# Attention and W1 of the next batch woven into the G2 matmuls of this batch, in one fixed order for all engines

## The chip, the core and the metric

The kernel runs on one core of one Trainium2 chip. The time is the device time of one execution in microseconds (us); several executions are taken and the median is quoted. The record gives with each run the span of the core, from its first to its last instruction, which is 1.7 to 1.9 us shorter than the time. Every ratio with an interval is the mean time of one kernel's fast runs over that of the other's fast runs of the same rounds, so it is not quite the ratio of the medians that stand beside it. A run over 1.5% above the fastest of its kernel counts as slow and is left out of the ratios.

In the profile's lines, PE is the TensorE matmul, PEld its weight load, DVE the VectorE, ACT the ScalarE, POOL the GpSimd and SP the SyncE. A "q" after an engine's name is its sequencer. L279 is line 279 of the kernel in question. PEclk is the granted TensorE clock as a share of full speed, and a "slot" is a stretch for which it was granted.

## The reference

Eight batches, eight heads, 512 rows of x and 32 rows of state per head, 64 values per row. Attention goes both ways between x and state (`xread`, `sread`). The heads are then concatenated to 512 columns, and every row goes through a two-layer network with SiLU.

```python
scores  = 0.125 * x @ state.T;  xread = softmax(scores)  @ state
scores2 = 0.125 * state @ x.T;  sread = softmax(scores2) @ x
x_moe = concat([xread, sread], axis=rows), heads side by side   # 8 * 544 rows x 512
h = x_moe @ w_in          # 512 x 2048
g = h * sigmoid(h)        # SiLU
out = g @ w_out           # 2048 x 512, float32
```

Both kernels use that xread of a batch is `a @ state`, with `a` the 512 x 32 softmax of a head. So `xread @ w_in` is `a @ (state @ w_in)`. The product W1 = state @ w_in (heads and state rows together: 256 rows x 2048 columns) is made once per batch; then G1 is a @ W1 with a contraction of 256 instead of 512, SiLU follows on ACT, and G2 is the product with w_out. The sread rows of all batches (256 rows) go through w_in directly, as one last group. W1 needs only state and w_in; it does not need the attention.

## The kernel before

It has two stages. The first does attention for 16 groups (a batch and half of its heads each) and W1 four groups later. The second does G1, SiLU and G2 for one batch after the other, with four output banks open at once. A scheduler orders the instructions.

```python
def c_part(b, hg, evict_split):                      # W1 of half a batch
    for fb in range(4):
        w1_psum = psC.tile([128, 512], FP32, tag="w1ps")
        for j in range(2):                           # two tiles of 64 columns
            nc.tensor.matmul(w1_psum[ds(64 * j, 64), :], stateT_bd[:, b, hg, j, :],
                w_in_sb[:, 2 * hg + j, ds(512 * fb, 512)], start=True, stop=True,
                tile_position=(0, 64 * j))
        ...                                          # eviction: 3 on DVE, 1 on ACT
for g, (b, hg) in enumerate(groups):                 # first stage
    ...   # load x, cast, transpose, scores, EXP, row sums, normalise on POOL, sread, transpose a
    if g >= 4:
        c_part(*groups[g - 4], evict_split=3)
        wout_quarter(g - 4, "pool")                  # cast of a piece of w_out
...
for b in range(B):                                   # second stage
    ...
    for ft in range(16):
        if ft + 1 < 16: emit_silu(ft + 1)
        if ft + 2 < 16: emit_G1(ft + 2)              # 2 matmuls of 512 columns
        emit_G2(ft)                                  # 4 matmuls of 512 columns, 4 banks
    ...                                              # evict and store
...
# the last group's stores: 4 batches outermost, then 32 rows
eng.dma_start(out_sread[ds(4 * tt, 4), ds(512, 32), :], out_sb[:])
```

The softmax here doesn't subtract the row's maximum and nothing guards it: scores larger than these inputs give would overflow.

Of the kernel before, what the change touches and what calls it, by code (L numbers as in the profile page):

```python
# [19 lines left out]
def kernel(  # L20
# [11 lines left out]
    B = 8  # L32
    H = 8
    S = 512
    NS = 32
    D = 64
    DM = 512
    DF = 2048
    SCALE = 0.125

    pers = ctx.enter_context(tc.tile_pool(name="pers", bufs=1))

    ident = pers.tile([128, 128], BF16)
    make_identity(nc, ident)

    stateT_bd = pers.tile([128, B, 2, 2, 64], BF16)
    w_in_sb = pers.tile([128, 4, DF], BF16)
    w_out_sb = pers.tile([128, 16, DM], BF16)
    aT_all = pers.tile([128, B, 2, S], BF16)
    xmoeT_sread = pers.tile([128, 4, B * NS], BF16)  # L50
    W1_sb = pers.tile([128, B, 2, DF], BF16)
    ones_sb = pers.tile([128, 1], BF16)
    nc.vector.memset(ones_sb[:], 1.0)

    win_stage = ctx.enter_context(tc.tile_pool(name="win_stage", bufs=1))
    win_tiles = []
    for kt in range(4):
        t = win_stage.tile([128, DF], FP32, tag=f"win{kt}")
        win_tiles.append(t)

    with tc.tile_pool(name="stA", bufs=1) as stA:
        state_stage = stA.tile([128, B, 2, D], FP32)
        state_nat = stA.tile([128, B, 2, D], BF16)

        for kt in range(4):
            for i in range(2):
                src = state[:, 2 * kt + i, :, :].rearrange("b ns d -> ns b d")
                eng = nc.sync if (2 * kt + i) % 2 == 0 else nc.scalar
                eng.dma_start(state_stage[ds(32 * kt, 32), :, i, :], src)

        for kt in range(4):
            nc.gpsimd.dma_start(win_tiles[kt][:], moe_w_in[ds(128 * kt, 128), :])

        nc.gpsimd.memzero(stateT_bd[:])

        nc.gpsimd.tensor_copy(state_nat[:], state_stage[:])  # L76

        with tc.tile_pool(name="psA", bufs=1, space=bass.MemoryType.PSUM) as psA:
            psum_st = psA.tile([128, B, 2, 2, 32], BF16)
            for b in range(B):  # L80
                nc.tensor.transpose(  # L81
                    psum_st[:, b, :, :, :],
                    state_nat[:, b, :, :],
                    ident[:],
                )
            nc.vector.tensor_copy(
                stateT_bd[ds(0, 64), :, :, :, ds(0, 32)],
                psum_st[ds(0, 64), :, :, :, :],
            )
            nc.scalar.activation(  # L90
                stateT_bd[ds(64, 64), :, :, :, ds(32, 32)],
                psum_st[ds(64, 64), :, :, :, :],
                func=COPY,
                bias=0.0,
            )

    groups = [(b, hg) for b in range(B) for hg in range(2)]
    wout_re = moe_w_out.rearrange("(gg q) m -> q gg m", q=128)

    with tc.tile_pool(name="poolB4", bufs=2) as poolB4, \  # L100
         tc.tile_pool(name="poolB2", bufs=2) as poolB2, \
         tc.tile_pool(name="wout_pool", bufs=2) as wout_pool, \
         tc.tile_pool(name="poolPB2", bufs=2, space=bass.MemoryType.PSUM) as poolPB2, \
         tc.tile_pool(name="poolPB1", bufs=1, space=bass.MemoryType.PSUM) as poolPB1, \
         tc.tile_pool(name="psC", bufs=2, space=bass.MemoryType.PSUM) as psC:

        wout_tiles = {}

        def c_part(b, hg, evict_split):
            for fb in range(4):  # L110
                w1_psum = psC.tile([128, 512], FP32, tag="w1ps")
                for j in range(2):
                    nc.tensor.matmul(  # L113
                        w1_psum[ds(64 * j, 64), :],
                        stateT_bd[:, b, hg, j, :],
                        w_in_sb[:, 2 * hg + j, ds(512 * fb, 512)],
                        start=True,
                        stop=True,
                        tile_position=(0, 64 * j),
                    )  # L120
                dst = W1_sb[:, b, hg, ds(512 * fb, 512)]
                if fb < evict_split:
                    nc.vector.tensor_copy(dst, w1_psum[:])  # L123
                else:
                    nc.scalar.activation(dst, w1_psum[:], func=COPY, bias=0.0)  # L125

        def wout_quarter(qidx, eng):
            g2, q = qidx // 4, qidx % 4
            if eng == "pool":
                nc.gpsimd.tensor_copy(w_out_sb[:, qidx, :], wout_tiles[g2][:, q, :])  # L130
            elif eng == "dve":
                nc.vector.tensor_copy(w_out_sb[:, qidx, :], wout_tiles[g2][:, q, :])
            else:
                nc.scalar.activation(
                    w_out_sb[:, qidx, :], wout_tiles[g2][:, q, :], func=COPY, bias=0.0
                )

        for g, (b, hg) in enumerate(groups):
            if g == 0:
                wout_tiles[0] = wout_pool.tile([128, 4, DM], FP32, tag="wout", name="wout0")  # L140
                nc.sync.dma_start(wout_tiles[0][:], wout_re[:, ds(0, 4), :])
            elif g == 2:
                wout_tiles[1] = wout_pool.tile([128, 4, DM], FP32, tag="wout", name="wout1")
                nc.scalar.dma_start(wout_tiles[1][:], wout_re[:, ds(4, 4), :])
            elif g == 8:
                wout_tiles[2] = wout_pool.tile([128, 4, DM], FP32, tag="wout", name="wout2")
                nc.sync.dma_start(wout_tiles[2][:], wout_re[:, ds(8, 4), :])
            elif g == 12:
                wout_tiles[3] = wout_pool.tile([128, 4, DM], FP32, tag="wout", name="wout3")
                nc.scalar.dma_start(wout_tiles[3][:], wout_re[:, ds(12, 4), :])  # L150

            if g < 4:
                nc.vector.tensor_copy(w_in_sb[:, g, :], win_tiles[g][:])  # L153

            x_stage = poolB4.tile([128, 2, 4, 2, D], FP32, tag="x_stage")
            x_nat = poolB4.tile([128, 2, 4, 2, D], BF16, tag="x_nat")
            xT_sb = poolB4.tile([128, 2, 4, 128], BF16, tag="xT_sb")
            exp_nat = poolB4.tile([128, 4, 2, 2, 32], BF16, tag="exp_nat")
            rowsumA = poolB4.tile([128, 4, 2, 2, 1], FP32, tag="rowsumA")
            recipA = poolB4.tile([128, 4, 2, 2, 1], FP32, tag="recipA")  # L160

            a_norm = poolB2.tile([128, 4, 2, 2, 32], BF16, tag="a_norm")
            recipB = poolB2.tile([128, 1], FP32, tag="recipB")
            sread_sb = poolB2.tile([128, D], BF16, tag="sread_sb")

            xT_psum = poolPB2.tile([128, 2, 4, 128], BF16, tag="xT_psum")
            scores_psum = poolPB2.tile([128, 4, 2, 2, 32], FP32, tag="scores_psum")
            sread4_psum = poolPB1.tile([128, 65], FP32, tag="sread4_psum")
            trans_psum = poolPB1.tile([128, 5, 2, 2, 32], BF16, tag="trans_psum")

            for hl in range(4):
                jj, ii = hl // 2, hl % 2
                h = 4 * hg + hl
                src = x[b, h].rearrange("(p c) d -> p (c d)", p=128, c=4)
                eng = nc.sync if hl % 2 == 0 else nc.scalar
                eng.dma_start(x_stage[:, jj, :, ii, :], src)

            nc.vector.tensor_copy(x_nat[:], x_stage[:])  # L178

            for j in range(2):  # L180
                for c in range(4):
                    nc.tensor.transpose(  # L182
                        xT_psum[:, j, c, :], x_nat[:, j, c, :, :], ident[:]
                    )

            nc.scalar.activation(xT_sb[:], xT_psum[:], func=COPY, bias=0.0)  # L186

            for c in range(4):
                for j in range(2):
                    nc.tensor.matmul(  # L190
                        scores_psum[:, c, j, :, :],
                        xT_sb[:, j, c, :],
                        stateT_bd[:, b, hg, j, :],
                        start=True,
                        stop=True,
                    )

            nc.scalar.activation(  # L198
# [78 lines left out]
    with tc.tile_pool(name="psD_h", bufs=3, space=bass.MemoryType.PSUM) as psD_h, \  # L277
# [8 lines left out]
        for b in range(B):  # L286
# [45 lines left out]
            for ft in range(16):  # L332
                if ft + 1 < 16:
                    emit_silu(ft + 1)
# [55 lines left out]
        for ft in range(16):  # L390
            if ft + 1 < 16:
                emit_silu_s(ft + 1)
            if ft + 2 < 16:
                emit_G1_s(ft + 2)
# [40 lines left out]
```

## Time and profile before

| what | value | read from |
|---|---|---|
| time | 307.87 us (three runs, 307.54 to 310.25) | runs |
| span of the profiled run | 311.4 us | page |
| attention and W1, 20 to 122 us | PE busy 73%, clock 0.72 | windows |
| G1 and G2, 123 to 301 us | PE busy 99%, clock 1.00 | windows |
| one 512-column matmul at full clock | 0.216 us from start to start | chain of waits |
| last matmul to end of span | 10.1 us | timeline |

The page of the kernel before: part 1 (busy time and share by engine), two rows of part 2 (40 slices of the span, in tenths) and part 4 (the chain that ended last).

```profile
PE 253.0 (81%) x1638; PEld 123.2 (40%) x1656; DVE 96.5 (31%) x217; ACT 121.7 (39%) x198; POOL 31.8 (10%) x40
...
PE   0015777777878797999999999999999999999960
...
PEclk9999759558655769999999999999999999999995
...
PE 71%; DMA 11%; DVE 5%; POOL 5%; issue 3%; ACT 2%; ACTq 1%; DVEq 0%; SPq 0%; POOLq 0%
```

The windows view of the kernel before, for the two stages. The columns are named in its first line.

```profile
core 0: us, PE busy (x) PEld busy (x) DVE busy (x) ACT busy (x) POOL busy (x), PEclk, DMA share, GB/s
20.00:122.00 102.00, 74.51 (x793) 39.53 (x795) 70.98 (x179) 40.52 (x55) 26.29 (x28) 0.72 0.46 109
123.00:301.00 178.00, 176.56 (x835) 82.75 (x852) 19.88 (x33) 80.43 (x142) 0.00 (x0) 1.00 0.14 48
```

The second stage is full: its time is its matmuls. The first is not: no engine is busy all the time, and where PE pauses, the clock granted to it falls as well, so even its busy time is inflated. What can be gained is in the first 122 us and in the end.

The PE timeline of the kernel before, near the end of the first stage, shows what a pair of W1 matmuls costs (start, duration, engine, line, operation, out<-in, shape, count).

```profile
117.41 0.41 PE L113 MATMUL w_psum<-w_in_sb,stateT_bd 128*64 128x512 bf16 x2
117.75 0.60 PE L298 MATMUL h_psum<-aT_all,W_sb 128*128 128x512 bf16 x2
```

The two W1 matmuls of a pair, on different column tiles, run at the same time; from the start of the pair to the next matmul are 0.34 us, of which 0.216 us is what one 512-column matmul takes; the other 0.12 us comes where the tile shape changes, as matmuls of one shape follow each other at 0.216.

### The profile page before, as it was taken

The page shows a single profiled execution, that of the slowest core. Times are in us where ns is not written, and L with a number is a line of the kernel's source. Part 1 is how long each engine was busy: PE and PEld are TensorE (multiplying, and loading weights), DVE is VectorE, ACT ScalarE, POOL GpSimd, SP SyncE. Part 2 cuts the span into 40 slices and gives each one's busy share as a digit, 9 for nine tenths or more (in the row PEclk, how much of TensorE's full clock was granted, in tenths as well). Part 3 has the DMA queues.
Part 4 walks back from the last instruction along what each step waited for, and adds up shares of the span by engine and source line. Part 5 has one row for each costly group of instructions (what it writes and reads, how often), then busy time and mean ns, then how long its engine had stood idle before and what let it go on. Part 6 is the DMA issues. An engine that isn't in the chain of part 4 may idle for free.

```text
span 311.4 us, 4295 instructions
## 1 busy us (share of the span) xinstructions
PE 253.0 (81%) x1638; PEld 123.2 (40%) x1656; DVE 96.5 (31%) x217; ACT 121.7 (39%) x198; POOL 31.8 (10%) x40
## 2 busy tenths in 40 slices
PE   0015777777878797999999999999999999999960
PEld 0012454443444432444444444444444444445640
DVE  0333677778766866003011030030110300301100
ACT  0021435325423352544435444444354444443430
POOL 5026433212212110000000000000000000000000
PEclk9999759558655769999999999999999999999995
DMA  7998746463533000004004030030030300300301
GB/s 212 378 348 214 163 107 155 98 202 84 119 87 68 2 1 0 0 2 137 0 2 135 0 115 22 0 135 2 1 135 0 119 18 0 137 0 0 138 3 64
DMA packets 43549, 26.50 MB, mean 85 GB/s; under 512 B 36616, under 2 KB 36616, under 8 KB 43016
## 3 DMA queue, kind: packets, MB, share of 16 engines
q1 hardware_dynamic: 21476, 11.01, 12.6%
q10 hardware_dynamic: 21476, 11.01, 12.5%
q0 software_dynamic: 576, 4.19, 3.7%
q8 instruction: 13, 0.21, 0.3%
q14 instruction: 8, 0.07, 0.1%
HBM read 17.30 MB, written 8.91 MB: 84 GB/s over the span
## 4 chain that ended last, share of the span: by engine, by line
PE 71%; DMA 11%; DVE 5%; POOL 5%; issue 3%; ACT 2%; ACTq 1%; DVEq 0%; SPq 0%; POOLq 0%
PE h_psum L298 18%; DMA x_stage<-in_x_dram 6%; PE w_psum L113 5%; DMA state_stage<-in_state_dram 5%; POOL a_norm L205 4%; PE xT_psum L182 2%; PE h_psum L356 2%; PE trans_psum L235 2%; DVE W_sb L123 2%; PE sread_psum L215 1%; PE out_psum_2497 L320 1%; PE out_psum_1539 L320 1%; PE out_psum_1697 L320 1%; PE out_psum_2017 L320 1%; PE out_psum_2177 L320 1%
## 5 line engine op out<-in xcount | busy, mean ns | idle before, releaser
L310 ACT ACTIVATE g_sb<-h_psum 128x512 bf16<-128x512 f32 x128 | 75.6, 597 | 88.1 <-PE h_psum L298 81.8
L298 PE MATMUL h_psum<-aT_all,W_sb 128*128 128x512 bf16 x251 | 74.7, 382 | 0.5 <-issue 0.3
L320 PEld LDWEIGHTS <-g_sb 128*128 128x128 bf16 x512 | 49.5, 98 | 62.1 <-ACT g_sb L310 2.6
L113 PE MATMUL w_psum<-w_in_sb,stateT_bd 128*64 128x512 bf16 x128 | 33.9, 529 | 7.0 <-ACT stateT_bd L90 4.1
L298 PEld LDWEIGHTS <-W_sb 128*128 128x128 bf16 x256 | 24.9, 98 | 31.6 <-issue 3.0
L123 DVE CAST W_sb<-w_psum 128x512 bf16<-128x512 f32 x48 | 31.9, 684 | 8.5 <-PE w_psum L113 7.9
L186 ACT ACTIVATE xT_sb<-xT_psum 128x1024 bf16<-128x1024 bf16 x16 | 16.4, 1024 | 30.5 <-PE xT_psum L182 21.4
L205 POOL TENSOR_TENSOR a_norm<-exp_nat,recipA 128x512 bf16<-128x512 bf16 x16 | 19.0, 1189 | 59.6 <-DVE sread_sb L246 33.8
L182 PE MATMUL xT_psum<-ident,x_nat 128*128 128x128 bf16 x128 | 16.1, 276 | 7.8 <-DVE x_nat L178 4.3
L235 PE MATMUL trans_psum<-ident,a_norm 128*128 128x128 bf16 x64 | 8.6, 280 | 11.8 <-POOL a_norm L205 11.8
L198 ACT ACTIVATE exp_nat<-scores_psum 128x512 bf16<-128x512 f32 x16 | 9.6, 598 | 17.0 <-PE scores_psum L190 11.5
L81 PE MATMUL psum_st<-ident,state_nat 128*128 128x128 bf16 x8 | 1.0, 311 | 18.2 <-POOL state_nat L76 18.2
L182 PEld LDWEIGHTS <-x_nat 128*128 128x128 bf16 x128 | 11.1, 124 | 11.2 <-DVE x_nat L178 7.1
L113 PEld LDWEIGHTS <-stateT_bd 128*64 128x64 bf16 x128 | 7.9, 121 | 16.2 <-issue 9.8
L125 ACT ACTIVATE W_sb<-w_psum 128x512 bf16<-128x512 f32 x16 | 9.5, 596 | 11.8 <-PE w_psum L113 9.6
L178 DVE CAST x_nat<-x_stage 128x1024 bf16<-128x1024 f32 x16 | 11.8, 735 | 5.8 <-DMA x_stage<-in_x_dram 5.7
L235 PEld LDWEIGHTS <-a_norm 128*128 128x128 bf16 x64 | 5.0, 120 | 18.1 <-POOL a_norm L205 17.9
L202 DVE TENSOR_REDUCE rowsumA<-exp_nat 128x16 f32<-128x512 bf16 x16 | 10.9, 681 | 1.8 <-ACT exp_nat L198 1.6
L190 PE MATMUL scores_psum<-stateT_bd,xT_sb 128*128 128x64 bf16 x128 | 9.2, 230 | 1.5 <-ACT xT_sb L186 1.4
L190 PEld LDWEIGHTS <-xT_sb 128*128 128x128 bf16 x128 | 7.3, 122 | 6.0 <-ACT xT_sb L186 3.6
L153 DVE CAST w_in_sb<-t 128x2048 bf16<-128x2048 f32 x4 | 4.9, 1227 | 15.2 <-DMA t<-in_moe_w_in_dram 15.2
L368 ACT ACTIVATE g_sb<-h_psum 128x256 bf16<-128x256 f32 x16 | 6.0, 384 | 8.9 <-PE h_psum L356 8.7
(102 smaller groups left out, 310.9 us busy)
## 6 DMA issues: line engine op xcount, KB each, us to landing
out_dram<-out_sb SPq DMA_DIRECT2D x17, 256.0 KB, 2.4
out_dram<-out_sb ACTq DMA_DIRECT2D x17, 256.0 KB, 2.5
t<-in_moe_w_in_dram POOLq DMA_DIRECT2D x4, 1024.0 KB, 11.9
x_stage<-in_x_dram SPq DMA_DIRECT2D x32, 128.0 KB, 3.2
x_stage<-in_x_dram ACTq DMA_DIRECT2D x32, 128.0 KB, 2.9
wout_273<-in_moe_w_out_dram ACTq DMA_DIRECT2D x1, 1024.0 KB, 20.8
wout_131<-in_moe_w_out_dram SPq DMA_DIRECT2D x1, 1024.0 KB, 20.3
wout_759<-in_moe_w_out_dram SPq DMA_DIRECT2D x1, 1024.0 KB, 5.8
```

The costliest lines, as they stand in the source:

```text
L113: nc.tensor.matmul(w1_psum[ds(64 * j, 64), :], stateT_bd[:, b, hg, j, :], w_in_sb[:, 2 * hg + j, ds(512 * fb, 512)], start=True, stop=True ...
L123: nc.vector.tensor_copy(dst, w1_psum[:])
L178: nc.vector.tensor_copy(x_nat[:], x_stage[:])
L182: nc.tensor.transpose(xT_psum[:, j, c, :], x_nat[:, j, c, :, :], ident[:])
L186: nc.scalar.activation(xT_sb[:], xT_psum[:], func=COPY, bias=0.0)
L190: nc.tensor.matmul(scores_psum[:, c, j, :, :], xT_sb[:, j, c, :], stateT_bd[:, b, hg, j, :], start=True, stop=True,)
L202: nc.vector.tensor_reduce(rowsumA[:], exp_nat[:], axis=AX, op=ADD)
L205: nc.gpsimd.tensor_tensor(a_norm[:], exp_nat[:], recipA[:].to_broadcast([128, 4, 2, 2, 32]), op=MULT,)
L235: nc.tensor.matmul(trans_psum[:, c, :, :, :], a_norm[:, c, :, :, :], ident[:], is_transpose=True, skip_group_check=True,)
L298: nc.tensor.matmul(h1_psum[:], W1_sb[:, b, hg, ds(128 * ft, 128)], aT_all[:, b, hg, :], start=(hg == 0), stop=(hg == 1), skip_group_check= ...
L310: nc.scalar.activation(g_sb[:], h1_tiles.pop(ft)[:], func=SILU, bias=0.0,)
L320: nc.tensor.matmul(out_psums[tt][:], g_sb[:, ds(128 * tt, 128)], w_out_sb[:, ft, :], start=(ft == 0), stop=(ft == 15), skip_group_check=True,)
```

## The change

The intent is to have no first stage. The order of every engine's instructions is fixed by hand. While G2 of batch k fills PE, the exps, row sums, W1 and transposes of batch k+1 and the transposes and scores of batch k+2 are put between its matmuls. G2 fills one output bank with 16 matmuls and then the next, so only two output banks are needed and the other six serve the woven work. Heads are taken in pairs on the contraction rows, so that W1 runs as eight tiles of 64 rows by 32 columns at once. The weights are cast to bfloat16 by the DMA. The sread rows are kept with the 32 rows outermost, so the last store has 32 rows outermost too.

The diff cut to its core; dropped lines of the old kernel were shown above.

```diff
+    def w1_m(b, j, bks):
+        for kt in range(KT):
+            for half in range(2):
+                nc.tensor.matmul(
+                    bank[bks[half]][ds(32 * kt, 32), :],
+                    sbd[ds(64 * half, 64), b, kt, half, :],
+                    w_in_sb[ds(64 * half, 64), kt, ds(512 * j, 512)],
+                    start=True, stop=True, skip_group_check=True,
+                    tile_position=(64 * half, 32 * kt),
+                )
+    def load_w(j):                      # float32 in HBM, bfloat16 in SBUF
+        nc.gpsimd.dma_start(w_in_sb[:, :, ds(512 * j, 512)], win_re[:, :, ds(512 * j, 512)])
+        nc.gpsimd.dma_start(w_out_sb[:, ds(4 * j, 4), :], wout_re[:, ds(4 * j, 4), :])
...
+        for i in range(5):              # start: batch 0, a quarter of the heads at a time
+            if i < 4:
+                cast_x(0, "dve", (i,))
+                x_T(0, i, XB[i])
+                x_Te(0, i, 1, XB[i], "act")
+            if i > 0:
+                sc(0, i - 1, SB[i - 1])
+                ex(0, i - 1, 1, SB[i - 1])
+                norm_s(0, i - 1, 1)
+                norm_m(0, "dve", i - 1, 1)
...
+        def exps(b):
+            ex(b, 0, 2, "a0")           # EXP on ACT
+            ex(b, 2, 2, "a1")
+            norm_s(b)                   # row sums and reciprocal on DVE
+            norm_m(b, "pool")           # normalise on POOL
...
+        def phase(k, fill, tts=(0, 1, 2, 3)):
+            for tt in tts:
+                bk = ("o0", "o1")[tt % 2]
+                for ft in range(16):
+                    g2(k, tt, ft, bk)
+                    for f in fill.get(16 * tt + ft, ()):
+                        f()
+                o_e(k, tt, bk)
...
+        for k in range(2, 7):           # the five steady batches
+            n = k + 1
+            fill = {}
+            exps(n)
+            if k + 2 < B:
+                load_x(k + 2, nc.sync)
+                cast_x(k + 2, "pool")
+            for j in range(4):
+                add(fill, 3 + 3 * j, L(W1x, n, j, ("w0", "w1"), ("dve", "dve")))
+            att_tail(fill, n, 15, 25, 21)        # sread, its transpose, transposes of a
+            for i in range(16):
+                add(fill, 25 + 2.3 * i, L(g1, n, i))
+            if k + 2 < B:
+                att_head(fill, k + 2, 42, 56)    # transposes of state and x; scores
+            phase(k, fill)
```

A "step" below is one of the 64 G2 matmuls of a batch. W1x is one group of eight W1 matmuls with the evictions of its two banks. Batches 0 and 1 have orders of their own, in the same style.

## The prediction

> **What bounds the kernel now.** It runs two stages in a row. The windows view shows attention plus W1 up to about 122 us: PE is busy only 52 to 83% of each 20 us stretch and is granted a clock of 0.50 to 0.88. From 123 to 301 us the G1/G2 stage runs with PE at 99% and clock 1.00: in the chain of waits 512-column matmuls follow each other every 0.216 us, so a batch (32 G1 + 64 G2) takes 20.7 us and eight take 166 us; the last group (sread rows) takes 14 us. The last 9.4 us (timeline) are two output stores, landing about 6 and 8 us after the last matmul, and about 1 us of teardown. The chain in the first 35 us is mostly DMA (state landing at 16.3 us, then x).
>
> **What the change does.** Attention and W1 of the next batch fill the same PE stream as G2, so the 122 us stage loses its own time and keeps only its PE time. Costs per steady batch at full clock, from gaps between matmul starts in the timeline: G2 13.8, G1 6.9, x transposes 16 x 0.056 = 0.9, scores 16 x 0.054 = 0.9, sread and row sums about 0.85 (16 started in 0.2 us), a transposes 0.5, W1 about 1.8. W1 is now eight 64x32 tiles at once per 512 columns; before, pairs already started 4 ns apart and took one 0.216 us slot, plus about 0.2 us for switching tile shapes in and out. I take 0.45 us per group of eight. Sum: 25.7 us per batch.
>
> Waits that I expect to stay, per steady batch: the exps (about 1.0 us each on ACT) come after the last SILU of the batch before; then DVE does the row sums (0.69 us per 512 elements, so about 1.2, plus 0.26) before the first W1 eviction. Meanwhile PE reaches the second W1 group and waits about 2.8 us; the third and fourth wait about 0.8 us each, because two banks take two DVE evictions (0.69 us, one per 0.6 us) per group. That is 4.4 us: 30 us per batch.
>
> Sum: start to the first G1 12 (x and the first state land by about 5, then the short attention chain); batch 0 about 34 (28 of PE, 6 of waits for banks) plus 2 for late weights; batch 1 39 (it also carries all G1 of batch 2); batches 2 to 5 30.3 each = 121; batch 6 28.5; batch 7 20.8; last group 7; end 4. The end shrinks because the last store has 32 rows outermost, not 4: the Trainium skill, "DMA: Bandwidth & Descriptors", on how many engines serve a DMA, says the outermost dimension sets that number (up to 16). Total 268 in the profile; unprofiled runs were 1.1% shorter (307.9 against 311.4).
>
> **Predicted: 265 us, range 249 to 283; faster by over 2% 0.97, within 2% 0.02, slower 0.01.**
>
> **What would show it.** Clock 1.0 in nearly all slices after the first; no 120 us stage; steady batches of about 30 us in the timeline; the PE waits named as DVE W1 evictions, the longest at the second W1 group of a batch; a W1 group of eight within about 0.5 us; first G1 near 12 us; under 5 us after the last matmul.
>
> **What would make it wrong.** Weights are now cast in the DMA on one queue, 8.4 MB: at the 380 GB/s of the first slices they land by about 28 us, at half that rate batch 0 stalls 10 us or more. If eight W1 tiles do not overlap, each batch costs 2 us more. If the row sums or exps end sooner, the waits shrink and 250 is reachable. If POOL slows DVE, or long PE waits lower the clock, it is over 275.

## The result, and the profile after

| | before | after |
|---|---|---|
| time, median | 309.06 us (four runs, 307.54 to 312.86) | 282.88 us (four runs, 282.39 to 283.39) |
| ratio of fast runs, 95% interval | | 0.913 (0.906 to 0.921) |
| span of the profiled run | 311.4 us | 281.5 us |
| mean granted clock, as recorded (see below) | 0.896 | 0.950 |
| recorded time at half clock up to the last matmul | 58 us | 27 us, in slots of 3.4 or 6.8 us |

The change is faster by 8.7%, and the time lies just inside the predicted range, at its upper end. The page after, the same parts:

```profile
PE 237.8 (84%) x1777; PEld 112.8 (40%) x1810; DVE 103.0 (37%) x194; ACT 120.1 (43%) x194; POOL 43.8 (16%) x81
...
PE   4359979996889778996989778996989698999994
...
PEclk9999997999899979997799979998899979999999
...
PE 71%; ACT 11%; DVE 10%; issue 5%; DMA 1%; ACTq 0%; POOL 0%; DVEq 0%
```

There is no empty stage any more. But the PE row dips once in every batch, and the clock row dips with it. ACT and DVE now hold 21% of the chain that ended last.

The first digits of the PEclk rows mislead. The clock record begins only at 24.8 us here, and at 31.9 us in the kernel before, and the page counts the time before it as full clock. But the spacing of matmuls in the timeline says otherwise:

```profile
19.65 2.34 PE L255 MATMUL ps_h<-aT,W 128*128 128x512 bf16 x5 [0.99 <-DVE W L79]
25.02 0.59 PE L279 MATMUL ps_o<-w_out_sb,g 128*128 128x512 bf16 x2
```

From 19.65 to 23.1 us matmuls of 512 columns start about 0.427 us apart, from 25.0 us on 0.216. So PE ran at half clock before the record began, in both kernels (the kernel before has 128-column transposes 0.107 us apart at 27 us, and 0.056 later), and the means and sums in the table leave that out.

The fourth output store of each batch gives the length of a batch. The sum of the prediction stands beside it.

| part | predicted us | measured us |
|---|---|---|
| start to the first G1 | 12 | 19.6 |
| batch 0, from there to its fourth store | 36 | 35.9 |
| batch 1 | 39 | 40.0 |
| batches 2 to 5 | 30.3 each | 31.5, 32.0, 31.3, 31.1 |
| batch 6 | 28.5 | 29.5 |
| batch 7 | 20.8 | 20.8 |
| last group | 7 | 6.7 |
| end | 4 | 3.2 |
| sum | 268 | 281.5 |

Now one steady batch (its predecessor's fourth store starts at 126.99 us). It is the one whose half-clock slot is 6.8 us long; in the others it is 3.4. The PE timeline after:

```profile
127.03 0.41 PE L234 MATMUL ps_w<-w_in_sb,sbd 64*32 64x512 bf16 x8
127.37 0.82 PE L279 MATMUL ps_o<-w_out_sb,g 128*128 128x512 bf16 x3
130.77 1.22 PE L234 MATMUL ps_w<-w_in_sb,sbd 64*32 64x512 bf16 x8 [2.58 <-DVE W L79]
131.92 1.46 PE L279 MATMUL ps_o<-w_out_sb,g 128*128 128x512 bf16 x3
133.31 0.70 PE L234 MATMUL ps_w<-w_in_sb,sbd 64*32 64x512 bf16 x8
134.33 1.06 PE L279 MATMUL ps_o<-w_out_sb,g 128*128 128x512 bf16 x2 [0.33 <-issue]
135.32 0.70 PE L234 MATMUL ps_w<-w_in_sb,sbd 64*32 64x512 bf16 x8
135.96 1.46 PE L279 MATMUL ps_o<-w_out_sb,g 128*128 128x512 bf16 x3
```

L234 is W1 and L279 is G2. A W1 group of eight takes 0.34 us until the next matmul. The second group waits 2.58 us, named as a W1 eviction on DVE. After it the G2 matmuls follow each other at 0.43 us instead of 0.216: the clock is at one half. The windows view of the same batch says so:

```profile
130.60:137.40 6.80, 6.29 (x37) 1.49 (x40) 4.57 (x8) 0.00 (x0) 4.46 (x9) 0.50 0.28 97
137.40:158.90 21.50, 20.59 (x164) 10.51 (x166) 6.11 (x12) 11.59 (x18) 0.00 (x0) 1.00 0.10 37
```

What DVE waited for before those evictions is in the timelines of ACT and of DVE:

```profile
125.47 0.60 ACT L263 ACTIVATE g<-ps_h 128x512 bf16<-128x512 f32 x1 [0.50 <-PE ps_h L255]
126.08 1.28 ACT L150 ACT_TABLE_LOAD   x1
127.38 1.09 ACT L150 ACTIVATE en<-ps_a 128x512 bf16<-128x512 f32 x2
```

```profile
128.56 1.22 DVE L160 TENSOR_REDUCE rs<-en 128x32 f32<-128x1024 bf16 x1 [1.60 <-ACT en L150]
129.81 0.35 DVE L161 RECIPROCAL rs<-rs 128x32 f32<-128x32 f32 x1
130.09 1.22 DVE L79 CAST W<-ps_w 128x512 bf16<-128x512 f32 x2
132.03 1.29 DVE L79 CAST W<-ps_w 128x512 bf16<-128x512 f32 x2 [0.73 <-PE ps_w L234]
```

The chain is: last SILU, table load (1.28 us), two exps (1.09 together), row sums (1.22), reciprocal (0.35), and only then the first W1 evictions, which the second W1 group of PE waits for. The prediction had this chain but for the table load. The Trainium skill, "ScalarE: Activation LUTs", says in the section "Step-by-step: what each stage is for" that the engine's active tables hold one set of functions at a time, and in "Table sets: the hidden batching unit" that calls should be batched by set. The kernel before did so without meaning to, as all exps came before all SILUs (its trace has two loads in all); the changed kernel alternates EXP and SILU once per batch. This trace agrees: it has seven loads before EXP, one for each of batches 1 to 7, and seven before SILU, 1283 ns each, besides two at the start:

```profile
L263 ACT ACT_TABLE_LOAD x7 | 9.0, 1283 | 60.7 <-PE ps_h L255 60.6
...
L150 ACT ACT_TABLE_LOAD x7 | 9.0, 1283 | 0.1
```

And the PE waits after in total (total us, number of times, longest):

```profile
PE ps_w L234 <- DVE W L79: 16.6, 12, 3.0
PE ps_w L128 <- DVE x_n L79: 4.5, 2, 2.3
PE ps_h L255 <- ACT g L263: 3.6, 5, 0.7
```

The third line is the other half of the table story: once in each of the five steady batches the third G1 waits 0.73 us for a bank, because the first SILU of the batch comes after a table load. From start to start it comes 1.11 us after the matmul before it, where 0.22 is usual, so the loss is 0.89 us.

### The profile page after: what moved, and what is told of

Its sections match the earlier page's. It is cut to its first block, busy times and chain, and to the rows that moved or that the text cites. A ratio compares the mean times of both kernels' runs of the same rounds, so it can differ in the third digit from the quotient of the medians.

```text
span 281.5 us, 4371 instructions
## 1 busy us (share of the span) xinstructions
PE 237.8 (84%) x1777; PEld 112.8 (40%) x1810; DVE 103.0 (37%) x194; ACT 120.1 (43%) x194; POOL 43.8 (16%) x81
## 4 chain that ended last, share of the span: by engine, by line
PE 71%; ACT 11%; DVE 10%; issue 5%; DMA 1%; ACTq 0%; POOL 0%; DVEq 0%
PE ps_o L279 33%; PE ps_h L255 19%; PE ps_w L234 4%; DVE W L79 3%; DVE rs L160 3%; ACT L150 3%; ACT en L150 3%; PE ps_w L279 3%; PE ps_h L266 2%; ACT g L263 2%; PE ps_a L128 2%; ACT L263 1%; PE ps_a L181 1%; DMA st_f<-in_state_dram 1%; PE ps_a L191 1%
## 5 line engine op out<-in xcount | busy, mean ns | idle before, releaser
L279 PE MATMUL ps_o<-w_out_sb,g 128*128 128x512 bf16 x458 | 137.4, 395 | 4.1 <-issue 2.2
L263 ACT ACTIVATE g<-ps_h 128x512 bf16<-128x512 f32 x128 | 75.4, 597 | 60.3 <-PE ps_h L255 56.5
L255 PE MATMUL ps_h<-aT,W 128*128 128x512 bf16 x246 | 74.8, 387 | 5.6 <-ACT g L263 3.6
L279 PEld LDWEIGHTS <-g 128*128 128x128 bf16 x512 | 47.6, 100 | 58.2 <-issue 14.8
L79 DVE COPY o_sb<-ps_o 128x512 f32<-128x512 f32 x30 | 20.5, 688 | 72.7 <-PE ps_o L279 72.7
L255 PEld LDWEIGHTS <-W 128*128 128x128 bf16 x256 | 24.7, 99 | 33.8 <-issue 7.7
L165 POOL TENSOR_TENSOR an<-en,rs 128x1024 bf16<-128x1024 bf16 x7 | 13.4, 1911 | 144.8 <-DVE rs L161 144.8
L79 DVE CAST W<-ps_w 128x512 bf16<-128x512 f32 x49 | 31.2, 678 | 12.5 <-PE ps_w L234 12.5
L263 ACT ACT_TABLE_LOAD x7 | 9.0, 1283 | 60.7 <-PE ps_h L255 60.6
L234 PE MATMUL ps_w<-w_in_sb,sbd 64*32 64x512 bf16 x200 | 17.6, 488 | 16.8 <-DVE W L79 16.6
L81 POOL CAST x_n<-x_f 128x256 bf16<-128x256 f32 x52 | 18.5, 407 | 25.1 <-DMA x_f<-in_x_dram 13.5
L234 PEld LDWEIGHTS <-sbd 64*32 64x32 bf16 x256 | 5.9, 92 | 39.5 <-issue 39.3
L160 DVE TENSOR_REDUCE rs<-en 128x32 f32<-128x1024 bf16 (+1 forms) x11 | 10.2, 929 | 25.0 <-ACT en L150 25.0
L128 PEld LDWEIGHTS <-x_n 128*128 128x128 bf16 x128 | 8.7, 102 | 9.4 <-DVE x_n L79 6.4
L279 PE MATMUL ps_w<-w_out_sb,g 128*128 128x512 bf16 x31 | 10.2, 412 | 0.1
L150 ACT ACT_TABLE_LOAD x7 | 9.0, 1283 | 0.1
L128 PE MATMUL ps_a<-ident,x_n 128*128 128x128 bf16 x112 | 8.3, 219 | 0.0
## 6 DMA issues: line engine op xcount, KB each, us to landing
st_nat<-in_state_dram POOLq DMA_DIRECT2D x7, 32.0 KB, 11.1
```

What stands on the lines that cost most here:

```text
L79: nc.vector.tensor_copy(dst, src)
L81: nc.gpsimd.tensor_copy(dst, src)
L128: nc.tensor.transpose(v[:, kt % 2, c, :], x_n[b % 2][:, kt, c, :, :], ident[:])
L150: nc.scalar.activation(en[b % 2][:, :, :, ds(kt, n), :].rearrange("p c h k s -> p k (c h) s"), v[:, ds(kt % 2, n)], func=EXP, bias=0.0, sc ...
L160: nc.vector.tensor_reduce(v, en[b % 2][:, :, :, ds(kt, n), :], axis=AX, op=ADD)
L165: e.tensor_tensor(an[b % 2][:, :, :, ds(kt, n), :].rearrange("p c h k s -> p (c h) k s"), en[b % 2][:, :, :, ds(kt, n), :].rearrange("p c ...
```

## The experiments

Eleven kernels ran. All gave correct results by the reference. Medians of four runs (six for casts_first); the batch length is the spacing of fourth stores in the profile, batches 3 to 5. They ran in three rounds on three chips, with the kernel before beside them but not the changed kernel again. So differences of 1 to 4 us against 282.9 compare different rounds; the intervals of such small gains overlap that of the changed kernel, and it is the profile that decides there. Two runs count as slow: one of evict_split (280.3) and one of silu_early (282.9). Without them the means are 276.7 and 279.4 us, so 6.1 and 3.5 us under 282.9.

| run | median us | change against 282.9 | batch us | ratio to before, 95% interval |
|---|---|---|---|---|
| the changed kernel | 282.9 | | 31.1 to 32.0 | 0.913 (0.906 to 0.921) |
| norm_late | 271.8 | -11.1 | 29.0 | 0.884 (0.874 to 0.893) |
| evict_split | 277.1 | -5.8 | 28.9 to 30.2 | 0.898 (0.889 to 0.907) |
| one_table | 265.6 | -17.3 | 28.3 | 0.861 (0.854 to 0.869) |
| unwoven | 316.0 | +33.1 | 37.7 to 37.9 | 1.025 (1.015 to 1.034) |
| casts_first | 282.9 | 0.0 | 30.9 | 0.915 (0.908 to 0.923) |
| before_store | 307.6 | (the kernel before) | | 0.993 (0.985 to 1.001) |
| warm_wait | 280.1 | -2.8 | 30.6 | 0.906 (0.900 to 0.912) |
| silu_early | 280.3 | -2.6 | 30.3 to 30.6 | 0.903 (0.894 to 0.912) |
| start_both | 279.2 | -3.7 | 31.1 to 31.9 | 0.904 (0.897 to 0.911) |
| w1_ahead | 255.2 | -27.7 | 25.5 | 0.825 (0.820 to 0.831) |
| best | 244.3 | -38.6 | 25.1 | 0.791 (0.784 to 0.799) |

### Does the weaving earn the gain? (unwoven)

```diff
-                add(fill, 3 + 3 * j, L(W1x, n, j, ("w0", "w1"), ("dve", "dve")))
-            att_tail(fill, n, 15, 25, 21)
+                add(fill, 0, L(W1x, n, j, ("w0", "w1"), ("dve", "dve")))
+            att_tail(fill, n, 0, 0, 0)
...
-                att_head(fill, k + 2, 42, 56)
+                # st_T, both xTs and both scs of batch k + 2, together at step 56
```

> In the five steady batches W1 and the tail of attention of the next batch stand together before the second G2 matmul, and the head of the batch after it stands together at step 56; the same instructions, not woven. If the weaving itself is what hides attention and W1, a batch costs 34.5 us or more instead of 31.3, more if the clock stays low after the long gap: total 298 to 312. If waits had already eaten what the weaving hides, the total stays below 290.

Measured 316.0 us, above the expected 298 to 312 and slower even than the kernel before. A steady batch takes 37.7 us, and the trace has 10.2 us at half clock in most steady batches (13.7 in the first). So the other parts of the change gain nothing without the weaving; against this order it is worth 33 us on five batches, some of it as clock. This order puts all of W1 in one place, with two banks for it; what a better unwoven order would lose was not run.

### The order on DVE, or the amount of its work? (norm_late, evict_split)

```diff
-            exps(n)
+            exps(n, False)                    # the two EXPs alone
...
             for j in range(4):
                 add(fill, 3 + 3 * j, L(W1x, n, j, ("w0", "w1"), ("dve", "dve")))
+                if j == 1:
+                    add(fill, 3 + 3 * j, L(norms, n))    # row sums, reciprocal, normalise
```

> In the five steady batches the row sums, reciprocals and normalisation of the next batch stand after the second W1 group instead of before the first. Theory A (order): the long PE wait of a batch, 2.75 us before the second W1 group, comes only from the row sums standing ahead of the first W1 evictions on DVE; then each batch loses about 3 us and the total falls from 283 to about 268. Theory B (amount): DVE has about 7.5 us of work (output eviction 0.7, row sums and reciprocal 1.6, eight W1 evictions 5) in a stretch where PE has only 4.4 us, so the wait only moves to the third and fourth group; what is gained is the 1.3 us of the first evictions that now run while ACT still computes exps: about 276.

The edit also puts POOL's cast of x of the batch after next behind the normalisation, which the text above does not say. It is no rival here: a W1 eviction on DVE takes 0.678 us in the mean in both runs.

Measured 271.8 us, between the two expectations. PE's waits for the evictions went from the 12 shown above to these:

```profile
PE ps_w L234 <- DVE W L79: 10.3, 23, 2.0
```

The long wait of a steady batch is gone (the longest gap between two matmul starts there fell from 2.96 to 1.28 us), but the sum of these waits fell only from 16.6 to 10.3 us: much of the wait only moved, as theory B says. What theory B had left out is the clock: with no long wait, no steady batch has a half-clock slot. A batch went from 31.3 to 29.0 us.

```diff
-                add(fill, 3 + 3 * j, L(W1x, n, j, ("w0", "w1"), ("dve", "dve")))
+                add(fill, 3 + 3 * j, L(W1x, n, j, ("w0", "w1"), ("dve", "act")))
```

> In the five steady batches the second of the two W1 evictions of a group goes to ACT, which is idle there. Theory B (amount of DVE work): the groups follow every 1.35 us instead of 2.0, about 2.5 us less per batch, total about 270. Theory A (order): the long wait for the row sums stays at about 2.3 to 2.7 us and only the short waits go, about 1.2 us per batch, total about 277.

Measured 277.1 us: the expectation of theory A. The profiled run of this kernel counts as slow (280.3 us, over 1.5% above the fastest run), so its details are used only roughly: the gap before the second W1 group is still 2.96 us in it, and the half-clock slots are still there in all steady batches but one. Relieving DVE after the long wait does not help against the wait itself. Neither theory alone was right: the order makes the long wait, the amount of work makes the ones after it.

### The table loads (one_table, silu_early)

```diff
-            func=EXP,
-            bias=0.0,
+            func=SILU,
+            bias=1.0,
             scale=SCALE,
```

> Not the function asked for: SILU of 1 + 0.125 s stands where EXP of 0.125 s stood, so that ACT never changes its table; all else is as in the changed kernel, and the result may be slightly off. Theory C: the 1.28 us table load before the exps of every batch delays the row sums and with them the W1 evictions, so that each of seven batches gets about 1.3 us shorter: total about 274. Rival: the loads lie where ACT is idle and cost nothing: 282 to 283.

Measured 265.6 us, 17.3 us less, about twice what was expected. (The result is not the function asked for; this is no kernel to use. The preloads of the two tables at the start are changed with it.) A steady batch fell by 3.0 us. Three things add up to that: the gap before the second W1 group, which the load before the exps had lengthened, fell from 2.96 to 1.54 us (1.4 us); the wait of the third G1 is gone (0.9 us from start to start), which I had not put into the expectation; and a rest of about 0.65 us I put down to the half clock, as all recorded slots at half clock but one, in batch 2, went too (warm_wait, below, finds 0.7 us for the clock alone). The second W1 group in one of its batches:

```profile
151.97 0.37 PE L234 MATMUL ps_w<-w_in_sb,sbd 64*32 64x512 bf16 x1 [1.16 <-DVE W L79]
```

```diff
             ex(b, 0, 2, "a0")
             ex(b, 2, 2, "a1")
+            nc.scalar.preload_act_table(SILU)
```

> One line more than the changed kernel: the SILU table is loaded right after the exps, while ACT has nothing to do, and no longer at the first SILU of the batch, where the third G1 waits 0.67 us for it. If that wait is on the path in batches 2 to 6 and once more in batch 1, the total falls by 3.5 to 4.5 us, to about 279. If it is made up later in the batch, 282 to 283. Together with what is left of the change to one table (17.3 us in all) this splits that gain into the load before the exps with its low clock, and the load before the SILUs.

(The 0.67 us of the text stands in no view; the trace has 0.73.) Measured 280.3 us, with runs from 277.5 to 282.9; the three fast runs have a mean of 279.4, 3.5 us less and so at the edge of the expectation, with a spread too wide to fix the size. In the profile the 0.7 us waits of G1 for ACT are gone and batches 2 to 5 are 1.0 us shorter in the mean.

### The clock (warm_wait)

```diff
+        def busy(m):
+            for _ in range(m):
+                nc.tensor.matmul(bank["h0"][:], zeros[:], w_out_sb[:, 0, :], start=True, stop=True, ...)
...
+            add(fill, 5, L(busy, 10))
             att_tail(fill, n, 15, 25, 21)
```

> The changed kernel with ten matmuls of 512 columns that nobody reads (2.2 us at full clock) put before the second W1 group of the five steady batches, where PE waits about 2.7 us. The wait stays, but PE is busy in it. Theory F: the half clock after the wait comes from the idle time, and about 1 us per batch of it is on the path: clock 1.0 in these batches, total 277 to 279. Rival 1: the half clock hides under the DVE evictions: clock 1.0, total 282 to 283. Rival 2: the clock falls because of the 64x32 matmuls, not the idle time: it stays at 0.5 in one slot per batch.

Measured 280.1 us, 2.8 us less and between theory F and rival 1, with ten matmuls more per batch that do nothing useful. The windows view of one of its batches:

```profile
126.00:136.00 10.00, 8.59 (x96) 3.47 (x98) 6.82 (x12) 1.38 (x3) 4.71 (x9) 1.00 0.44 133
```

The clock is 1.00 through the stretch where the changed kernel had 0.50. So the idle time lowers the clock, not the shape of the W1 matmuls, which are the same here. The half clock cost 0.7 us per batch (31.3 to 30.6), less than I thought; I take it that most of it lay under the DVE evictions that PE had to wait for anyway. Where a slot falls matters too: in the profile of casts_first (below), with the same steady batches, they take 30.9 us, and against that the clock is worth 0.3.

### The start (casts_first, start_both)

The first G1 came 7.6 us later than predicted. In the DVE order of the changed kernel, the cast of a quarter of x stands behind the normalisation of the quarter two before, which waits for PE and ACT to finish that quarter, so the quarters follow each other at 3.1 us. The PE timeline of the changed kernel shows the last two:

```profile
9.95 0.61 PE L128 MATMUL ps_w<-ident,x_n 128*128 128x128 bf16 x4 [2.16 <-DVE x_n L79]
13.08 0.61 PE L128 MATMUL ps_w<-ident,x_n 128*128 128x128 bf16 x4 [2.31 <-DVE x_n L79]
```

```diff
+        for i in range(4):
+            cast_x(0, "dve", (i,))
         for i in range(5):
             if i < 4:
-                cast_x(0, "dve", (i,))
                 x_T(0, i, XB[i])
```

> Only the start differs: DVE casts all four quarters of x of batch 0 before the first row sums, where the changed kernel puts the cast of a quarter behind the normalisation of the quarter two before. Theory D (DVE order makes the start late): the four quarters no longer follow each other at 3.1 us, the first G1 comes at about 15.5 us instead of 19.6, total about 279. Rival: the weights land too late (second quarter of w_in at 16.3 us, of w_out at 18.8) and batch 0 waits for them instead: total 282 or more.

The first G1 came at 15.1 us, 4.5 us earlier, and the total did not move (282.9). The fourth store of batch 0 came at 55.5 us, the same as before this edit. The PE waits and the DVE timeline of this run show where it went:

```profile
PE ps_a L128 <- DVE x_n L79: 3.5, 2, 3.1
```

```profile
33.13 1.71 DVE L79 CAST x_n<-x_f 128x256 bf16<-128x256 f32 x4 [10.37 <-DMA x_f<-in_x_dram]
```

The first transposes of batch 1 (L128) wait for the cast of its x, and that for the load, which is issued at 22.8 us but lands only at 33.0, after the weights (landing until 30.6), which were issued before it. In the changed kernel it was issued at 27.8 us and landed at 33.5, unnoticed, as PE came just late enough. Nobody waited for the weights themselves.

```diff
         for i in range(4):
             cast_x(0, "dve", (i,))
+        gate(1)                       # a one-element write that holds the load back until here
+        load_x(1, nc.sync)
...
-            gate(1)
-            load_x(1, nc.sync)
```

> As the run with the casts of batch 0 first, which made the first G1 4.5 us earlier and the total no shorter, and in addition the load of x of batch 1 is released right after those casts, not after the second W1 group. Theory G: the earlier start was lost because the first transpose of batch 1 then waited 3.1 us for that load, which queued behind the weights until 33 us; with it early, PE keeps the 4 us and the total is 278 to 280. Rival: the load now delays the weights, and G1 or G2 of batch 0 waits for them: total above 281.

Measured 279.2 us, 3.7 us less, and the fourth store of batch 0 at 51.6 instead of 55.5 us. Theory G holds. The first half of the remedy alone gave nothing; the second alone was not run.

### The end (before_store)

```diff
-    xmoeT_sread = pers.tile([128, 4, B * NS], BF16)
+    xmoeT_sread = pers.tile([128, 4, 2, NS, 4], BF16)
...
-            eng.dma_start(out_sread[ds(4 * tt, 4), ds(512, 32), :], out_sb[:])
+            eng.dma_start(out_sread[ds(512, 32), ds(4 * tt, 4), :], out_sb[:])
```

> The kernel before, with the sread rows kept in the order of the changed kernel, so that the last two stores have 32 rows outermost instead of 4. Theory E: the outermost dimension sets how many engines serve a store; the last stores land about 2.5 us after issue instead of 5 to 8 and the kernel before gets 5 to 6 us shorter, ratio about 0.98. Rival: the landing is slow for another reason and nothing changes, ratio 1.00.

The profile agrees: from the last matmul to the end of the span are 4.6 us instead of 10.1, and the store on the SP queue lands 2.4 us after its issue. The waits of the SP queue of the kernel before, for its last two stores (L430 is the end of the program):

```profile
SPq L430 <- DMA out_dram<-out_sb: 7.7, 2, 5.2
```

of this run:

```profile
SPq L430 <- DMA out_dram<-out_sb: 2.3, 2, 1.6
```

and of the changed kernel, whose last store has 32 rows outermost as well:

```profile
SPq L569 <- DMA out_dram<-o_sb: 0.7, 1, 0.7
```

In the times of all runs the two count as the same: 307.6 against 309.8 us, ratio 0.993 (0.985 to 1.001), while 0.98 was expected. The kernel before scatters by as much as the effect. So the landing time is shown, and what it is worth over many runs stays open: between nothing and 4.6 us by the interval.

### A better version (w1_ahead, best)

As W1 needs no attention, it need not stand in the same crowded stretch as the row sums. This version makes W1 of batch k+2 during batch k, spread over the batch.

```diff
-            for j in range(4):
-                add(fill, 3 + 3 * j, L(W1x, n, j, ("w0", "w1"), ("dve", "dve")))
-            att_tail(fill, n, 15, 25, 21)
+                for j, s in enumerate((6, 29, 37, 53)):
+                    add(fill, s, L(W1x, k + 2, j, ("w0", "w1"), ("dve", "dve")))
+            att_tail(fill, n, 15, 26, 23)
             for i in range(16):
-                add(fill, 25 + 2.3 * i, L(g1, n, i))
+                add(fill, 28 + 2.2 * i, L(g1, n, i))
...  # state is transposed a batch earlier, W1 of batch 3 put into batch 1;
...  # and the edits of silu_early and casts_first
```

> A version meant to be better: W1 of a batch, which needs nothing of the attention, is woven one batch earlier and spread over the batch, so no W1 group waits for row sums or for the group before; the SILU table is loaded right after the exps; the casts of batch 0 come first. If the waits of the changed kernel are those of order and of the amount of DVE work in one short stretch, the steady batch falls from 31.3 to 25.6 to 26.5 us, clock 1.0, and the total to 249 to 254. If DVE or POOL work in the rest of the batch now binds, batches stay above 27.5 and the total above 258.

Measured 255.2 us, just over the expected range. The steady batch fell to 25.5 us, about as expected; batch 1 stayed at 40.9 us and the earlier start was lost, as in casts_first. The last version mends these:

```diff
+        # the edit of start_both, and in the first ten steps of batch 1:
+            if ft in (4, 6, 9):
+                W1x(2, (4, 6, 9).index(ft), ("w0", "w1"), ("dve", "dve"))
-            att_tail(fill, n, 15, 26, 23)
+            att_tail(fill, n, 15, 27, 25)
-                add(fill, 28 + 2.2 * i, L(g1, n, i))
+                add(fill, 29 + 2.17 * i, L(g1, n, i))
```

> All that helped: W1 a batch ahead and spread, the SILU table loaded early, casts first with x of batch 1 early, W1 of batch 2 spread over the first part of batch 1, and the transposes of a two G2 steps later, for the 0.6 us that they waited for POOL. Expected 4 us less at the start, 3 in batch 1 and 0.3 in each steady batch against the version with W1 a batch ahead (255.2): 246 to 250. If the early x delays the weights it stays at 251 or more.

Measured 244.3 us, just under the expected range; ratio to the kernel before 0.791. It beats both kernels. As these edits were put in together, their shares of the last 11 us are not taken apart. Its page, in the rows shown before:

```profile
PE 223.9 (92%) x1779; PEld 109.6 (45%) x1810; DVE 100.7 (42%) x194; ACT 120.4 (50%) x194; POOL 43.6 (18%) x81
...
PE   3579988999889999999999999999999999999993
...
PEclk9999997999999999999999999999999999999999
```

Its PE timeline in a steady batch has no waits of note:

```profile
115.23 0.41 PE L234 MATMUL ps_w<-w_in_sb,sbd 64*32 64x512 bf16 x8
115.58 2.12 PE L279 MATMUL ps_o<-w_out_sb,g 128*128 128x512 bf16 x8
117.62 0.42 PE L191 MATMUL ps_a<-x_n,en 128*32 128x64 bf16 x32
117.97 0.35 PE L202 MATMUL ps_a<-ones,en 128*128 128x1 bf16 x8
118.19 2.32 PE L279 MATMUL ps_o<-w_out_sb,g 128*128 128x512 bf16 x9
```

A steady batch takes 25.1 us, and the prediction's sum of PE work alone was 25.7. DVE and ACT do the same work as in the changed kernel; only where it stands is different.

## Why the prediction was right or wrong

The direction was right, the range held (249 to 283, measured 282.9), and the middle was 18 us too low. Point by point:

- **"that 122 us stage loses its own time and keeps only its PE time"**: right. The run unwoven shows that the gain rests on it: in the lumped order of that run the kernel is slower than the kernel before.
- **"Sum: 25.7 us per batch"** of PE work: right, by the best version's 25.1 us. The eight W1 tiles do run at once; a group took 0.34 us, where I had put 0.45.
- **"PE reaches the second W1 group and waits about 2.8 us"**: right in place and size (2.58 us idle, 2.96 us from start to start), but by two errors that cancel. I had put the exps at "about 1.0 us each"; the two take 1.09 us together, as each handles 512 elements and not 1024. And I had overlooked the table load of 1.28 us. The run one_table removes that load, and the wait shrinks. The step that failed is the list of what the change adds: it had no table loads, because the diff shows none. They follow from the order of EXP and SILU on ACT. They also cost at a second place, 0.9 us at the first SILU of a batch. All in all they were worth 17.3 us, the low clock that they led to included.
- **"Clock 1.0 in nearly all slices"**: wrong. A slot of 3.4 or 6.8 us at half clock stood in each of batches 0 to 6. The prediction named this only as a risk. By warm_wait it was worth 0.7 us per steady batch on the path (0.3 against casts_first). Besides, PE ran at half clock until about 24.8 us, which the clock record does not show.
- **"the third and fourth wait about 0.8 us each"**: not seen as such. At half clock the G2 matmuls between the groups took so long that PE arrived when the banks were free or nearly so (waits of at most 0.22 us). I take the time as lost either way. Steady batches came to 31.1 to 32.0 us instead of 30.3, in sum 4.8 us more for the four.
- **"start to the first G1 12"**: wrong by 7.6 us. I added the stages of a pipeline that I took to overlap; in DVE's order they do not. But the runs casts_first and start_both show that the sum of stages is the wrong picture here: with the first G1 earlier by 4.5 us, the load of x of batch 1 was next in line and nothing was gained, until it was moved too. Of the 7.6 us, the order on DVE explains those 4.5; the other 3.1 (15.1 against 12) no run took apart, and the half clock of the start is in them.
- **"plus 2 for late weights"**: the weights landed at 29.2 us, close to the 28 given for full rate, and nobody waited for them. That batch 0 still took the 36 us forecast is luck: the 2 us of this wait did not come, and half clock, until 24.8 us and for 3.4 us from 41.9, which had not been counted, did. The cost of their transfer lay elsewhere, in what queued behind them.
- **"end 4"**: right in the profile (3.2).
- **"unprofiled runs were 1.1% shorter"**: this correction was wrong. The profile of the kernel before was of a long execution, and the prediction took its excess for a cost of profiling. Each run's time is 1.7 to 1.9 us longer than its span, the profiled run too (283.3 against 281.5 us). So of the 18 us, 13.5 are in the sum for the profile (268 against 281.5), 3 come from this subtraction, and the rest is that the time is longer than the span.

What stays open: how much of the 17.3 us of the table loads is clock and how much is wait in batches 0 and 1, as only the steady batches were taken apart; what is left of the late start; and what the faster end is worth over many runs.

## What to carry to other kernels

Weaving pays by keeping the bottleneck engine fed, but it also brings together on the other engines what stages had kept apart: ask of each of them what now alternates (tables), what now stands in line ahead of what the bottleneck waits for, and how much work falls in one short stretch. Move first what depends on least; here W1 needed no attention and moving it a batch ahead removed waits, low clock and crowding together. When an earlier start gains nothing, look for the next arrival in line before giving the idea up.

## What the Trainium skill lacked or had wrong

- "ScalarE: Activation LUTs", section "What ACT_TABLE_LOAD costs": the load of 1283 ns agrees to the nanosecond (seven and seven loads here). The page adds a drain of about 1380 ns, 2.66 us per switch; in this trace a SILU ended at 126.07 us, the load ran from 126.08, and the exp started at 127.38, so the whole switch took 1.3 us.
- "TensorE: Matmul & The Clock Gate", section "Back-to-back issue gap": it gives about 131 ns per 512-column matmul in a stream of weight loads and matmuls, and about 216 ns for an isolated one. Here the stream itself, each matmul with its own weights, ran at 216 ns, and 128-column transposes at 56 ns, where the page has 81.
- The same page, sections "HAM oscillation — how this bites in real kernels" and "Why this matters for your kernels": it tells to avoid PE gaps over about 3.4 or 3 us. Here shorter ones were followed by half clock for 3.4 us or more: 2.58 us of idle time in each of batches 3 to 6 of the changed kernel, 1.7 us in batch 0 of the best version, 1.6 us in batch 2 of one_table. But not always: 1.7 us in batch 0 of norm_late was not followed by it, nor was 2.58 us in one batch of evict_split. The idle times of 1.2 us in batches 3 to 6 of one_table never were. What decides in between, the runs do not show.
- "DMA: Bandwidth & Descriptors", section "Why a DMA increments its semaphore by 16 and not by 1", on how many engines serve a DMA: the traces agree. With 4 outermost, the ends of the two last stores were seen about 6.1 and 8.4 us after issue, with 32 (before_store) 2.4 and 2.8 us; and among the semaphore updates that each store left in the trace, 4 came at its landing with 4 outermost, and 16 with 32. No page has a rate for casting DMAs: 8.4 MB of float32 weights landed between 4.25 us (first issue) and 29.24 us, which is 336 GB/s on the reading side; the page of the profile counts them by the bytes written, half of that.
